# Program order for the way in of every batch, and the second batch's fold on GpSimd, in a long-convolution and mixture-of-experts kernel

## The chip, the core and the metric

The kernel runs on one core of a Trainium2 chip. The metric is the device time of one execution in microseconds (us). The kernel is one launch; its time before the change is the median of three runs.

## The reference

Four batches of 10048 positions and 128 channels go through a gated long convolution, and the result of all 40192 positions goes through a two-level mixture of experts. Cut to what matters:

```
u = x * v
h = (relu(pos_emb @ w1) @ w2) * exp(-0.01 * pos)          # the filter, one per channel
y = irfft(rfft(u, 2S) * rfft(h, 2S), 2S)[:, :S]           # causal convolution over positions
rows = (x * y).reshape(B * S, D)
# mixture of experts: 4 groups x 4 experts, hidden width 1024
g = argmax(rows @ w_group);  e = argmax(rows @ w_expert[g])
out[row] = p(g) * p(e) * (relu(rows @ w1[g, e]) @ w2[g, e])
```

All inputs and outputs are float32.

## The kernel before

The Fourier transforms are written as matrix products over a factorized length, so that TensorE does them. A loop `b = 0 … 4` runs over the batches, and each turn has two stages.

The **row stage** of turn `b` does two things side by side. The *way in* is the forward transform of batch `b`: 43 parts of 3 channels (42 of 3, one of 2). For each part SyncE loads a tile `xv` that holds x and v (288 KB, line 454), VectorE multiplies them in place (`product`, line 459), the halves `lo` and `hi` of the product are folded into `eo` = (lo + hi, lo − hi) (`fold`), 24 matmuls make `psa` from `eo` (line 406), and ScalarE copies `psa` out as `z` and `zr` (line 417). The *way out* is the inverse transform of batch `b − 1`: groups of 12 channels are transposed by TensorE (`pt`, lines 693 and 696), copied by ScalarE (`tt`, line 698), multiplied (`po`, lines 708 and 729), copied by ScalarE (`oo`, lines 738 and 739), then VectorE makes `yt` (line 744) and, with the loaded gate `xo`, `xy` (line 746). One group of 12 channels together with four parts of the way in is called a cycle here; a stage has 10.67 cycles. Turn 0 has only a way in, turn 4 only a way out. Turns 1, 2 and 3 have both; their row stages are called stage 1, 2 and 3.

The **middle** of turn `b` then multiplies batch `b`'s spectrum by the filter's, frequency by frequency: `psb` (TensorE), products `t` on VectorE (lines 654, 657), sum and difference `y` on GpSimd (lines 655, 658), `pbp` on TensorE (line 670).

Into turns 2, 3 and 4 the routing of earlier rows is woven: many small VectorE operations (lines 759 to 1050) that find each row's place, and row scatters on GpSimd (`prow`, line 372), with clears of unused places (line 387). GpSimd's scatters and clears are made to wait for a recent ScalarE copy, which paces them. After turn 4 come the experts' matmuls, which sort no further rows.

The fold of batch 0 is two GpSimd operations, or one on GpSimd and one on VectorE. For batches 1 to 3 ScalarE first writes −hi behind hi into the `xv` tile (line 470), and then one VectorE operation over 384 columns makes both halves (line 472):

```
both = self.minus.pop(d0)
nc.scalar.activation(both[:, :, 128:192], hi, AF.Copy, scale=-1.0)
signed = both[:, :, 64:192].rearrange("p d (j q) -> p d j q", j=2)
nc.vector.tensor_tensor(eo..., bc(lo, 2, 2), signed, ALU.add)
```

The source runs the products three to four parts and the folds three parts ahead of the matmuls (`run_ahead`, `AHEAD = 3`). There are 5 tiles for loads (`NLOAD`) and 5 for `eo` (`NPROD`). So a load for a part can start when the fold of the part five before it has read its tile.

The order of instructions on each engine comes from a scheduler, which places an operation by its own priorities and not where the source has it. `in_turn` overrides it: an operation given to it is kept on its engine right behind the operation that the source wrote before it. It adds an order, no wait. Before, this holds for batch 0 alone.

Of the kernel before, what the change touches and what calls it, by code (L numbers as in the profile page):

```python
# [15 lines left out]
AF = mybir.ActivationFunctionType  # L16
ALU = mybir.AluOpType
# [107 lines left out]
def bc(ap, axis, n):  # L125

    ap = ap.unsqueeze(axis)
    shape = list(ap.shape)
    shape[axis] = n
    return ap.broadcast_to(shape)  # L130
# [18 lines left out]
class Kernel:  # L149
# [280 lines left out]

    def in_turn(self, b, ins):

        if b == 0:
            self.tc.keep_in_program_order(ins)

    def product(self, b, d0, n):
# [25 lines left out]
    def fold(self, xt, b, d0, n):  # L462

        nc = self.nc
        eo = self.ap.tile([NR, GD, 128], F32, tag="prod", name="eo", bufs=NPROD)
        lo, hi = xt[:, :, 0:64], xt[:, :, 64:128]
        odd = d0 // GD % 2
        if b:
            both = self.minus.pop(d0)
            nc.scalar.activation(both[:, :, 128:192], hi, AF.Copy, scale=-1.0)  # L470
            signed = both[:, :, 64:192].rearrange("p d (j q) -> p d j q", j=2)
            nc.vector.tensor_tensor(
                eo[:, :n].rearrange("p d (j q) -> p d j q", j=2), bc(lo, 2, 2), signed, ALU.add
            )
            return b, eo, d0, n, False

        self.in_turn(b, nc.gpsimd.tensor_tensor(eo[:, :n, 0:64], lo, hi, ALU.add))
        sub = nc.vector if d0 >= FIRST and odd else nc.gpsimd
        self.in_turn(b, sub.tensor_tensor(eo[:, :n, 64:128], lo, hi, ALU.subtract))
        return b, eo, d0, n, d0 // GD % 5 == 4 or d0 // GD == 41  # L480
# [968 lines left out]
```

## Time and profile before

| what | before |
|---|---|
| median of three runs | 2063.18 us (2059.78 to 2067.74) |
| the profiled execution's own time | 2065.51 us |
| its span, first to last instruction | 2063.6 us |
| TensorE busy | 1919.7 us, 93% of the span |
| VectorE, ScalarE, GpSimd busy | 78%, 70%, 64% |
| stages 1, 2, 3 (249.98 to 358.21, 462.31 to 579.15, 690.98 to 809.53) | 108.23, 116.84, 118.55 us |
| the middles behind them | 104.10, 111.83, 102.63 us |
| last way out and experts (from 912.16) | to the end of the span |

The stages are read from the first transpose or the last back product of one stretch to that of the next. PE is TensorE, PEld its weight loads, DVE is VectorE, ACT is ScalarE, POOL is GpSimd, SP is SyncE; a "q" behind the name is the engine's own queue of DMA issues. The rows name a waiting instruction, then what it waited for.

### The profile page before, as it was taken

How to read it: one execution, taken by the hardware profiler on the slowest of the kernel's cores; microseconds unless marked ns; L12 is line 12 of the kernel's file. 1: busy time of each engine (PE TensorE's matmuls, PEld its weight loads, DVE VectorE, ACT ScalarE, POOL GpSimd, SP SyncE). 2: the span in 40 equal slices, each digit the busy share in tenths (PEclk: the TensorE clock that was granted, in tenths of full speed). 3: DMA queues.
4: the chain of work that ended last, by engine and by line, in shares of the span. 5: the costliest groups of instructions: out<-in, count | busy, mean ns of one | idle time of the engine just before them, and what ended most of it. 6: DMA issues, size and time to landing. Idle time of an engine off the chain costs nothing.

```text
span 2063.6 us, 53237 instructions
## 1 busy us (share of the span) xinstructions
PE 1919.7 (93%) x17518; PEld 1764.7 (86%) x17518; DVE 1604.0 (78%) x3462; ACT 1441.7 (70%) x3395; POOL 1320.7 (64%) x1371
## 2 busy tenths in 40 slices
PE   8988988977899789988899999999999999999997
PEld 7867877766777577767699999999999999999997
DVE  5587765687558875794699998889999998888885
ACT  6652377436743476446687888888888888888886
POOL 3247600674689657977167777888888885555554
PEclk9999999999999899999899999999999999999999
DMA  4699955976899578968444445455555544444442
GB/s 137 225 264 260 286 159 171 329 237 173 224 308 297 165 211 268 338 204 272 166 144 136 141 151 158 150 191 163 154 163 153 166 144 128 135 124 124 129 124 65
DMA packets 258717, 388.71 MB, mean 188 GB/s; under 512 B 32679, under 2 KB 132754, under 8 KB 258432
## 3 DMA queue, kind: packets, MB, share of 16 engines
q1 hardware_dynamic: 225024, 317.84, 51.3%
q0 software_dynamic: 23904, 51.83, 7.1%
q10 hardware_dynamic: 9504, 15.54, 2.7%
q8 instruction: 142, 2.33, 0.5%
q14 instruction: 143, 1.17, 0.2%
HBM read 303.08 MB, written 83.04 MB: 187 GB/s over the span
## 4 chain that ended last, share of the span: by engine, by line
PE 66%; DMA 8%; DVE 8%; POOL 5%; issue 4%; ACT 4%; SPq 1%; ACTq 0%; DVEq 0%; POOLq 0%
PE py L1318 7%; PE ph L1299 7%; PE ph L1297 7%; PE py L1316 7%; PE py L1317 7%; PE ph L1298 7%; PE psb L488 6%; DMA xv<-xv_in 5%; PE pbp L670 4%; PE psa L406 2%; PE ptm L1330 2%; PE px L1254 2%; PE ptr L811 2%; PE plt L819 1%; PE pt L696 1%
## 5 line engine op out<-in xcount | busy, mean ns | idle before, releaser
L1306 DVE SCALAR_TENSOR_TENSOR hl<-ph,hh 128x512 fp32r<-128x512 f32 x656 | 445.2, 683 | 93.4 <-ACT hh L1305 92.8
L1305 ACT ACTIVATE hh<-ph 128x512 fp32r<-128x512 f32 x656 | 395.7, 603 | 138.6 <-PE ph L1299 73.6
L372 POOL DMA_INDIRECT prow<-stg,adr x316 | 348.0, 1101 | 137.5 <-issue 60.2
L1342 POOL DMA_INDIRECT out<-os,to x328 | 349.0, 1064 | 91.5 <-issue 71.7
L1316 PE MATMUL py<-hh,wh 128*128 128x256 f32 x1312 | 398.6, 304 | 0.0
L1297 PE MATMUL ph<-xh,wh 128*128 128x256 f32 x1312 | 373.6, 285 | 5.1 <-DVE hl L1306 2.7
L1318 PE MATMUL py<-hh,wl 128*128 128x256 f32 x1312 | 373.2, 284 | 5.5 <-POOL wl L1286 5.5
L1299 PE MATMUL ph<-xh,wl 128*128 128x256 f32 x1312 | 373.5, 285 | 0.4 <-DVE wl L1286 0.4
L1298 PE MATMUL ph<-xl,wh 128*128 128x256 f32 x1312 | 373.0, 284 | 0.0
L1317 PE MATMUL py<-hl,wh 128*128 128x256 f32 x1312 | 371.4, 283 | 0.0
L1286 POOL TENSOR_TENSOR wl<-ws,wh 128x512 fp32r<-128x512 f32 x162 | 221.1, 1365 | 203.5 <-ACT wh L1279 202.3
L1318 PEld LDWEIGHTS py<-hh,wl 128*128 128x128 f32 x1312 | 251.4, 192 | 8.4 <-POOL wl L1286 8.3
L1297 PEld LDWEIGHTS ph<-xh,wh 128*128 128x128 f32 x1312 | 252.9, 193 | 5.8 <-ACT hh L1305 2.8
L1299 PEld LDWEIGHTS ph<-xh,wl 128*128 128x128 f32 x1312 | 253.3, 193 | 0.9 <-DVE wl L1286 0.8
L1298 PEld LDWEIGHTS ph<-xl,wh 128*128 128x128 f32 x1312 | 253.2, 193 | 0.1
L1317 PEld LDWEIGHTS py<-hl,wh 128*128 128x128 f32 x1312 | 252.7, 193 | 0.0
L1316 PEld LDWEIGHTS py<-hh,wh 128*128 128x128 f32 x1312 | 252.0, 192 | 0.0
L1286 DVE TENSOR_TENSOR wl<-mw,wh 128x512 fp32r<-128x512 f32 x328 | 237.3, 724 | 0.0
L655 POOL TENSOR_TENSOR y<-t 128x256 f32<-128x256 f32 (+1 forms) x160 | 120.1, 751 | 156.2 <-DVE t L654 152.0
L1279 ACT CAST wh<-mw 128x512 fp32r x328 | 206.6, 630 | 0.0
L1279 ACT CAST wh<-ws 128x512 fp32r<-128x512 f32 x328 | 205.6, 627 | 1.4 <-DMA ws<-m_w 1.4
L670 PE MATMUL pbp<-y,bp 128*128 128x256 f32 x632 | 169.7, 394 | 26.2 <-POOL y L658 25.6
(237 smaller groups left out, 4094.6 us busy)
## 6 DMA issues: line engine op xcount, KB each, us to landing
ws<-m_w SPq DMA_DIRECT2D x328, 256.0 KB
ht<-hspec SPq DMA_DIRECT2D x156, 256.0 KB
xv<-xv_in SPq DMA_DIRECT2D x131, 288.0 KB
bt<-c_b SPq DMA_DIRECT2D x95, 256.0 KB
xg<-prow SPq DMA_DIRECT2D x164, 130.0 KB
bp<-c_bp SPq DMA_DIRECT2D x76, 256.0 KB
stg<-xyd SPq DMA_DIRECT2D x76, 256.0 KB
xyd<-xy SPq DMA_DIRECT2D x57, 256.0 KB
```

The lines of the kernel that those rows point to most:

```text
L372: ins = self.nc.gpsimd.indirect_dma_start(self.d["prow"], bass.IndirectOffsetOnAxis(ap=u.adr[:, t : t + 1], axis=0), u.rows[:, t - u.t0], ...
L1279: k.fix(k.nc.scalar.copy(hi, self.matrix(i, half, self.ea)))
L1286: ins = v.tensor_tensor(lo, self.matrix(i, half, self.ed), self.wh[i][half].bitcast(F32), ALU.subtract)
L1297: k.fix(nc.tensor.matmul(ph[:, j], wh, self.xh, start=True, stop=False))
L1298: k.fix(nc.tensor.matmul(ph[:, j], wh, self.xl, start=False, stop=False))
L1299: k.fix(nc.tensor.matmul(ph[:, j], wl, self.xh, start=False, stop=True))
L1305: k.fix(nc.scalar.activation(hh, ph, AF.Relu))
L1306: k.fix(nc.vector.scalar_tensor_tensor(hl, ph, 0.0, hh.bitcast(F32), ALU.max, ALU.subtract))
L1316: k.fix(nc.tensor.matmul(self.py, wh, self.hh[c], start=(c == 0), stop=False))
L1317: k.fix(nc.tensor.matmul(self.py, wh, self.hl[c], start=False, stop=False))
L1318: k.fix(nc.tensor.matmul(self.py, wl, self.hh[c], start=False, stop=(c == NC - 1)))
L1342: ins = k.nc.gpsimd.indirect_dma_start(k.d["out"], bass.IndirectOffsetOnAxis(ap=self.to[:, h : h + 1], axis=0), o[:, h], None, bounds_chec ...
```

## The change

`in_turn` keeps program order for every batch, and not for batch 0 alone (the filter's own way in stays out). So the products and the copies `z` and `zr` of batches 1, 2 and 3 are now pinned. For batch 1 the fold becomes two GpSimd operations of 96 × 192 each (86 in all), with no ScalarE negation and no VectorE fold. For batches 2 and 3 the fold stays as it was, and its two operations are pinned too.

```diff
@@ in_turn
-        if b == 0:
+        if b != "h":
             self.tc.keep_in_program_order(ins)
@@ fold
+        if b == 1:
+            nc.gpsimd.tensor_tensor(eo[:, :n, 0:64], lo, hi, ALU.add)
+            nc.gpsimd.tensor_tensor(eo[:, :n, 64:128], lo, hi, ALU.subtract)
+            return b, eo, d0, n, False
         if b:
             both = self.minus.pop(d0)
-            nc.scalar.activation(both[:, :, 128:192], hi, AF.Copy, scale=-1.0)
+            self.in_turn(b, nc.scalar.activation(both[:, :, 128:192], hi, AF.Copy, scale=-1.0))
             signed = both[:, :, 64:192].rearrange("p d (j q) -> p d j q", j=2)
-            nc.vector.tensor_tensor(
+            ins = nc.vector.tensor_tensor(
                 eo[:, :n].rearrange("p d (j q) -> p d j q", j=2), bc(lo, 2, 2), signed, ALU.add
             )
+            self.in_turn(b, ins)
             return b, eo, d0, n, False
```

From the fold on, lines of the changed kernel are 5 higher (`yt` is line 749, `xy` 751, `tt` 703, `oo` 743 and 744); VectorE's fold moves from 472 to 476, the negation from 470 to 474, and GpSimd's new operations are lines 469 and 470.

**VectorE in the steady part of stage 2.** Numbers mark the tiles: `xv_6584` is a part's load tile, `eo` its fold. Before:

```order
761 L459 TENSOR_TENSOR xv_6584<-xv_6584 96x3x128
762 L472 TENSOR_TENSOR eo_6549<-xv_6522 96x384
763 L459 TENSOR_TENSOR xv_6632<-xv_6632 96x3x128
764 L459 TENSOR_TENSOR xv_6687<-xv_6687 96x3x128
765 L459 TENSOR_TENSOR xv_6708<-xv_6708 96x3x128
766 L744 TENSOR_TENSOR yt_6519<-po_6488,oo_6516 128x474
767 L472 TENSOR_TENSOR eo_6587<-xv_6546 96x384
768 L746 TENSOR_TENSOR xy1_5766<-yt_6519,xo_6502 128x79x6
769 L472 TENSOR_TENSOR eo_6635<-xv_6584 96x384
770 L472 TENSOR_TENSOR eo_6690<-xv_6632 96x384
```

The same place after the change:

```order
711 L459 TENSOR_TENSOR xv_6419<-xv_6419 96x3x128
712 L476 TENSOR_TENSOR eo_6422<-xv_6381 96x384
713 L459 TENSOR_TENSOR xv_6470<-xv_6470 96x3x128
714 L476 TENSOR_TENSOR eo_6473<-xv_6419 96x384
715 L749 TENSOR_TENSOR yt_6519<-po_6488,oo_6516 128x474
716 L751 TENSOR_TENSOR xy1_5766<-yt_6519,xo_6502 128x79x6
717 L459 TENSOR_TENSOR xv_6522<-xv_6522 96x3x128
718 L476 TENSOR_TENSOR eo_6525<-xv_6470 96x384
```

Before, three products stand in a row ahead of `yt`, and the folds that free load tiles stand behind it. After, product and fold alternate, and around the same `yt_6519` the products stand at an earlier part (`xv_6470` where `xv_6708` stood).

**ScalarE in a cycle of stage 1.** Before, from one set of `tt` copies to the `oo` copies of the same cycle:

```order
L698 COPY tt<-pt 128x512 x3
L470 ACTIVATE xv<-xv 96x3x64 x2
L417 COPY z<-psa 128x128x3
L417 COPY zr<-psa 128x3x30
L724 DMA xo<-x_out 128x474
L470 ACTIVATE xv<-xv 96x3x64 x2
L724 DMA xo<-x_out 128x474
L738 ACTIVATE oo<-po 64x474
```

After:

```order
L703 COPY tt<-pt 128x512 x3
L729 DMA xo<-x_out 128x474
L417 COPY z<-psa 128x128x3
L417 COPY zr<-psa 128x3x30
L743 ACTIVATE oo<-po 64x474
```

The negations are gone from stage 1, and with them ScalarE's waits on products there.

**GpSimd where the middle of turn 0 ends and stage 1 starts** (a piece of the difference; `y` is the middle's last sum and difference, `wr` to `iota` are four small constant loads):

```order
 L663 TENSOR_TENSOR y<-t_2945 128x2x128
+L469 TENSOR_TENSOR eo<-xv 96x3x64
 L660 TENSOR_TENSOR y<-t_2957 128x128
+L470 TENSOR_TENSOR eo<-xv 96x3x64
+L469 TENSOR_TENSOR eo<-xv 96x3x64
 L663 TENSOR_TENSOR y<-t_2960 128x128
 L193 DMA wr<-w_router 128x32
```

Three of the new operations stand ahead of the last `y`, on which the stage's first transposes depend.

**VectorE where stage 2 starts, after the change** (lines 955 to 983 are routing, in four passes; in the third and fourth, lines 964 to 977 between 961 and 981 run on GpSimd, so that line 981 waits for GpSimd):

```order
L981 TENSOR_REDUCE other<-f 128x79
L983 TENSOR_TENSOR pos<-pos,other 128x79
L955 SCALAR_TENSOR_TENSOR f<-keep,oh 128x316
L956 TENSOR_TENSOR oh<-oh,c_5586 128x4
L459 TENSOR_TENSOR xv<-xv 96x3x128 x5
L476 TENSOR_TENSOR eo<-xv 96x384 x4
L749 TENSOR_TENSOR yt<-po,oo 128x474
```

Before the change these five products stand one by one among the routing operations ahead of this place; now they stand together behind them.

## Rows read from the trace of the kernel before

**Rows 1.** The page: lines on the chain that ended last, with shares.

```profile
PE py L1318 7%; PE ph L1299 7%; PE ph L1297 7%; PE py L1316 7%; PE py L1317 7%; PE ph L1298 7%; PE psb L488 6%; DMA xv<-xv_in 5%; PE pbp L670 4%; PE psa L406 2%; PE ptm L1330 2%; PE px L1254 2%; PE ptr L811 2%; PE plt L819 1%; PE pt L696 1%
```

**Rows 2.** Windows: stages 1 to 3: us, PE, PEld, DVE, ACT, POOL busy, clock, DMA, GB/s.

```profile
249.98:358.21 108.23, 94.03 (x1442) 83.20 (x1441) 66.00 (x122) 84.23 (x212) 1.47 (x3) 0.98 0.62 169
...
462.31:579.15 116.84, 98.95 (x1442) 86.12 (x1441) 73.33 (x157) 84.25 (x210) 67.89 (x72) 0.93 0.73 205
...
690.98:809.53 118.55, 105.08 (x1444) 90.02 (x1444) 79.72 (x181) 83.08 (x210) 72.22 (x74) 0.89 0.71 204
```

**Rows 3.** Windows of single cycles: one of stage 1, three of stage 2.

```profile
303.12:311.76 8.64, 8.63 (x137) 7.65 (x135) 5.05 (x10) 6.92 (x19) 0.00 (x0) 1.00 0.71 195
...
480.92:495.86 14.94, 10.16 (x137) 8.62 (x136) 10.16 (x27) 11.46 (x30) 3.26 (x3) 0.77 0.59 175
495.86:505.16 9.30, 8.64 (x137) 7.66 (x136) 5.07 (x10) 5.55 (x15) 4.37 (x6) 1.00 0.86 226
505.16:519.61 14.45, 10.16 (x137) 8.64 (x136) 7.66 (x15) 10.48 (x26) 7.88 (x9) 0.88 0.73 192
```

**Rows 4.** Waits in stage 2: us in total, times, longest.

```profile
DVE xv L459 <- DMA xv<-xv_in: 28.2, 24, 3.0
ACT xv L470 <- DVE xv L459: 20.9, 19, 4.4
...
PE pt L696 <- ACT tt L698: 17.7, 9, 4.8
```

**Rows 5.** Waits in stage 1.

```profile
DVE xv L459 <- DMA xv<-xv_in: 28.5, 31, 3.0
ACT xv L470 <- DVE xv L459: 18.9, 22, 1.8
...
PE pt L696 <- ACT tt L698: 13.2, 8, 2.2
```

**Rows 6.** SyncE's own waits, stage 1 (line 454 issues the loads).

```profile
SPq L454 <- DVE eo L472: 71.9, 30, 5.8
...
SPq L454 <- DMA xv<-xv_in: 1.4, 1, 1.4
```

**Rows 7.** Timeline of stage 2: start, us, engine, line, operation, [idle before <- releaser].

```profile
507.42 0.55 DVE L459 TENSOR_TENSOR xv<-xv 96x384 f32<-96x384 f32 x1 [2.71 <-DMA xv<-xv_in]
...
510.61 1.50 ACT L698 COPY tt<-pt 128x384 f32<-128x384 f32 x3
...
511.16 1.02 PE L696 MATMUL pt<-ident,z 128*128 128x128 f32 x4 [4.29 <-ACT tt L698]
...
514.01 0.55 DVE L472 TENSOR_TENSOR eo<-xv 96x384 f32<-96x384 f32 x1 [1.41 <-PE psa L406]
...
518.44 0.55 DVE L459 TENSOR_TENSOR xv<-xv 96x384 f32<-96x384 f32 x1 [2.59 <-DMA xv<-xv_in]
```

**Rows 8.** Groups by line and shape over the span: busy us, mean ns | idle before.

```profile
L459 DVE TENSOR_TENSOR xv<-xv 96x384 f32<-96x384 f32 x126 | 71.8, 570 | 75.0 <-DMA xv<-xv_in 74.1 <-issue 0.4
L472 DVE TENSOR_TENSOR eo<-xv 96x384 f32<-96x384 f32 x126 | 70.0, 566 | 23.5 <-PE psa L406 16.7 <-POOL y L658 4.3 <-ACT xv L470 2.4
...
L470 ACT ACTIVATE xv<-xv 96x192 f32<-96x192 f32 x126 | 45.3, 365 | 74.8 <-DVE xv L459 68.5 <-issue 1.7 <-ACT zr L417 1.4
...
L477 POOL TENSOR_TENSOR eo<-x 96x192 f32<-96x192 f32 x37 | 26.6, 733 | 21.7 <-DVE x L459 20.5 <-PE psa L406 1.2
...
L746 DVE TENSOR_TENSOR xy<-yt,xo 128x474 f32<-128x474 f32 x60 | 38.9, 648 | 0.9
...
L477 POOL TENSOR_TENSOR eo<-xv 96x192 f32<-96x192 f32 x5 | 3.0, 590 | 0.0
```

**Rows 9.** Timeline, GpSimd, where stage 3 starts.

```profile
683.10 1.38 POOL L387 DMA_INDIRECT prow<-empty,fidx  x1 [2.47 <-ACT xv L470]
684.50 4.74 POOL L658 TENSOR_TENSOR y<-t 128x128 f32<-128x128 f32 x1
```

**Rows 10.** Timeline, TensorE, the last back product ahead of stage 3.

```profile
689.30 1.22 PE L670 MATMUL pbp<-y,bp 128*128 128x256 f32 x2 [7.89 <-POOL y L658]
```

## Prediction

> **What bounds the kernel now.** The page's chain is mostly TensorE, but one link is of another kind: 5% of the span, some 103 us, runs through the load of `xv` [rows 1]. Those loads belong to the way in of turns 0 to 3, so the place to look is the three stages in which a way in and a way out run side by side. The windows of these stages show TensorE busy for 94.03 of 108.23, 98.95 of 116.84 and 105.08 of 118.55 us [rows 2]: 14, 18 and 13.5 us idle, and in the later two some more lost because the granted clock falls (0.93, 0.89). One cycle undisturbed takes 8.64 us with TensorE busy for 8.63 of it; in stage 2 cycles of 14.94 and 14.45 us alternate with one of 9.30 [rows 3]. In the long ones TensorE's own work has grown to 10.16 us, the same 137 matmuls at a clock of 0.77 or 0.88: it first waits, then runs slowly.
>
> What it waits for is in the waits: TensorE's `pt` waits for ScalarE's `tt`, 17.7 us in stage 2; ScalarE's negation waits 20.9 us for VectorE's product, and the product 28.2 us for its load [rows 4]. Read from the bottom up that is one chain, since ScalarE works in order: a negation that waits holds up the `tt` copies behind it. Stage 1 shows the same with 13.2, 18.9 and 28.5 us [rows 5]. The timeline of one long cycle has it in sequence: the product at 507.42 came 2.71 us late, the `tt` copies started at 510.61, and `pt` resumed at 511.16 after 4.29 us [rows 7].
>
> Is the load late because the DMA is slow or because it is issued late? SyncE, which issues the loads, spends 71.9 us of stage 1 waiting for VectorE's fold (line 472), which frees a load tile, and 1.4 us for an earlier load [rows 6]. In the timeline a fold runs at 514.01 and the product at 518.44 gets its data after waiting 2.59 us [rows 7]: 4.4 us from a freed tile to a used one. So the tile is freed too late. VectorE's order explains it: three products stand in a row, each needing a new tile, while the folds that would free tiles stand behind them and behind `yt`.
>
> **The change part by part.**
>
> *Products and folds in program order (batches 2, 3).* It adds no operation and no wait. Product and fold alternate, so each freed tile is followed by its load, which now has about four parts, one cycle of 8.64 us [rows 3], until its product: twice the 4.4 us that it takes. I expect the product's waits for its load to go, with them most of the negation's and `pt`'s. What is late next: in order, `yt` waits for `oo`, and a product behind it waits too, but it is ahead by three parts. The DMA share rises: the same bytes in 102 instead of 116.84 us make 0.84 of 0.73 [rows 2]. A cycle with 0.86 ran in 9.30 us [rows 3], so I take not 8.64 but 9.2 us a cycle: 10.67 × 9.2 = 98.2 us. Bounds: 8.64 a cycle (92.2) and the mean of a long and a short cycle, (14.45 + 9.30) / 2 = 11.9, nothing gained.
>
> *The start of stages 2 and 3.* Before, the first five products and folds lay under the end of the middle, among routing. Now VectorE has the five products together behind its routing, and the first four folds behind them, so the way in starts later: five products and a first fold of 0.57 us [rows 8] are 3.4 us, unless the way out's own transposes cover them. I take +3.5 us in stage 2 (from +1 to +10). In stage 3 the first matmuls of the way in stand still further back, so +5 (from +2 to +10). So stage 2 becomes 98.2 + 3.5 = 101.7, that is −15; stage 3 98.2 + 5 = 103.2, −15.
>
> *Batch 1's fold on GpSimd.* It removes 43 ScalarE negations of 365 ns, 15.7 us, and 43 VectorE folds of 566 ns, 24.3 us [rows 8], and adds 86 GpSimd operations. An operation of this shape on `xv` takes 590 ns with no neighbour on VectorE and 733 ns beside VectorE's products [rows 8]: 50.7 to 63.0 us of GpSimd, which had 1.47 us in this stage [rows 2]. So GpSimd has room. ScalarE falls from 84.23 to about 68.5 us, and no longer stands between a product and `tt`, so `pt`'s 13.2 us of waits [rows 5] should mostly go. I take 9.0 us a cycle, 96 us, and 4 us at the start (three of the new operations stand ahead of the last `y`, 3 × 0.59 = 1.8 us, and I add as much again for the other folds, which the four constant loads hold up): 100 us, −8. Bounds: 92.2 + 2 = 94 and 108.
>
> GpSimd and VectorE slow each other, and this decides how good that is. `y` (128 × 128) took 4.74 us at 684.50 [rows 9] where VectorE ran operations with two inputs one behind the other; and 590 became 733 ns. If they exclude each other fully, the demand in stage 1 is 86 × 590 ns + 43 products × 570 ns + 22 `xy` × 648 ns = 50.7 + 24.5 + 14.3 = 89.5 us of 100 [rows 8]: it fits, without much to spare. This is where the Trainium skill speaks against the change: "SBUF — State Buffer", section "Who interferes with whom", says that a VectorE operation with two inputs in SBUF and a GpSimd operation that reads SBUF use one port pair, of which the first to issue holds the whole. The trace agrees (4.74 us for `y`). By that rule alone the sum is the 89.5 us just worked out, under the stage's 100, and stage 1 keeps its gain.
>
> *Ends of the middles.* At the start of stage 3 the last `y` stands on GpSimd behind a clear that came 2.47 us late, then starves itself [rows 9]; TensorE stood for 7.89 us [rows 10]. After the change the products and folds of the next batch no longer crowd VectorE there, so the `y` should take near its usual time of under a microsecond: 4 us. I count −3 for both ends together (from 0 to −7), since part of it is the late start counted above.
>
> **The sum.** −8 − 15 − 15 − 3 = −41. The profiled execution took 2065.51 us, so 2024.5. The median of the runs is 2.33 us lower (2063.18): about 2022. What comes after the last stage keeps its order and its time. 0.5% is 10.3 us.
>
> **The rivals.**
>
> *A: stage 1 gains nothing and the starts eat more.* If GpSimd is slowed to the 733 ns and VectorE is held in turn, the demand is 63.0 + 24.5 + 14.3 = 101.8 us in stage 1 plus the lags between product and fold: 108 as before, no gain; with starts of +6.5 and +8, stages 2 and 3 gain 12 each. With nothing from the middles' ends that is −24: 2041.5, or about 2039 as a median. For it: batch 0's folds on GpSimd took 733 ns beside products [rows 8]. Against it: GpSimd may lag by three parts before a matmul waits.
>
> *B: the load is slow by itself.* Then an earlier issue helps little, the product's waits of 28 us a stage [rows 4, 5] stay, and only the middles' ends gain: 2063.18 − 4, about 2059, no change that can be measured. For it: the DMA share is 0.73 in stage 2 [rows 2], and shorter stages push it up. Against: SyncE's own waits [rows 6].
>
> *C: slower, by the starts of stages 2 and 3.* VectorE is strictly in order there. Its routing waits for GpSimd, GpSimd's clears wait for a ScalarE copy (2.47 us here for a negation [rows 9]), and ScalarE's first copies of the new stage wait for matmuls whose folds now stand behind that routing. In such a ring nothing overlaps; a start then costs the whole middle's end again, the 7.89 us [rows 10] plus 3.4 and the clears' 1.38 each [rows 9], some 13 us for each of two stages, 26 in all. It decides the sign where the steady cycles gain less than that together; with a third of the forecast's 41 us, 14, it gives 2063 + 26 − 14 = 2075. Against: the first `tt`, `po` and `oo` of the way out need none of this.
>
> **How the numbers follow.** The forecast, about 2022, has a chance of 0.62; A 0.20, B 0.10, C 0.08. Better than forecast is bounded by 8.64 us a cycle and small starts: 92.2 + 2 in stage 1, 92.2 + 1 and + 2 in the others, −14 − 23.6 − 24.4 = −62, or 2001. The range of 2000 to 2051 takes in the forecast and A and leaves out B and C, together 0.18. Faster by over 0.5% has the forecast and A, 0.82; within 0.5% is B, 0.10; slower is C, 0.08.
>
> **What would show it.** Right: stages of about 100, 102 and 103 us; the product's waits for its load under 10 us a stage; no wait of `pt` for `tt` over 1 us in the steady part; granted clock near 1.0 in stages 2 and 3; GpSimd's folds between 590 and 733 ns. Wrong in the first step: product waits near 28 us with loads issued a cycle ahead (B). Wrong on stage 1: `psa` waiting for GpSimd's folds throughout (A). Wrong on the starts: TensorE idle for over 10 us where stages 2 and 3 begin (C). It would be faster than I think if the clock stays full and the middles, which I leave as they are, gain as well.

## The result and the profile after

The change took the median from 2062.12 us (2059.78 to 2067.74, four runs) to 2030.48 us (2027.63 to 2035.0, four runs): a ratio of 0.9845, 95% interval 0.9816 to 0.9873. 31.6 us were gained where 41 were forecast; the span fell from 2063.6 to 2030.3 us. The sign and the mechanism of the steady part held; one term of the sum was badly wrong, and it hides behind a total that looks nearly right.

The windows of the profile after, by nearly the same marks as [rows 2] and with the middles between them, have the columns us, PE, PEld, DVE, ACT and POOL busy with instructions, clock, DMA share, GB/s:

```profile
248.64:346.72 98.08, 97.30 (x1443) 84.59 (x1443) 49.10 (x80) 72.17 (x172) 56.26 (x87) 0.98 0.66 180
346.72:446.45 99.73, 92.15 (x575) 73.70 (x576) 80.71 (x191) 39.69 (x93) 68.28 (x91) 0.97 0.87 288
446.45:552.70 106.25, 98.26 (x1442) 86.26 (x1442) 77.15 (x152) 82.76 (x216) 65.61 (x71) 0.97 0.83 233
552.70:659.95 107.25, 94.09 (x577) 73.20 (x578) 82.56 (x188) 40.21 (x94) 93.50 (x120) 0.98 0.89 292
659.95:779.00 119.05, 108.81 (x1445) 93.53 (x1445) 84.46 (x182) 82.27 (x214) 67.09 (x73) 0.89 0.75 207
```

Read against the stages of before, 108.23, 116.84 and 118.55 us, and the middles of 104.10 and 111.83:

| part | before | after | gained | forecast |
|---|---|---|---|---|
| stage 1 | 108.23 | 98.08 | 10.2 | 8 |
| stage 2 | 116.84 | 106.25 | 10.6 | 15 |
| stage 3 | 118.55 | 119.05 | −0.5 | 15 |
| middles of turns 1 and 2 | 104.10, 111.83 | 99.73, 107.25 | 9.0 | 3 |
| all before, between and behind these | 1504.05 | 1499.94 | 4.1 | 0 |

The last row is the span less the others; of its 4.1 us 1.3 lie ahead of stage 1 and 2.8 behind stage 3. The marks differ a little: before, stages 1 and 2 start at the first `psa`, after the change at the last back product. From the first transpose to the middle's first `psb`, the marks used below, stage 1 gained 9.6 and stage 2 11.1 us. So stage 1 and the steady parts are as forecast or better, the middles' ends gave three times what was forecast, and stage 3 gave nothing. Single cycles in the steady part of stages 1, 2 and 3, by the windows of the profile after:

```profile
295.30:304.35 9.05, 9.05 (x137) 7.85 (x136) 4.93 (x9) 6.69 (x16) 5.36 (x8) 1.00 0.70 184
500.81:509.88 9.07, 8.89 (x137) 7.92 (x136) 6.19 (x12) 8.29 (x22) 7.08 (x9) 1.00 1.00 289
745.56:754.59 9.03, 9.03 (x137) 7.85 (x136) 6.63 (x14) 6.98 (x20) 6.45 (x8) 1.00 0.95 263
```

All three are alike, 137 matmuls in 9.03 to 9.07 us at the full clock, where [rows 3] had 14.94 and 9.30 in turn. In stage 2 the waits that [rows 4] showed are nearly gone:

```profile
ACT xv L474 <- DVE xv L459: 10.7, 6, 5.9
...
PE pt L701 <- ACT tt L703: 1.6, 5, 0.5
...
DVE xv L459 <- DMA xv<-xv_in: 0.8, 2, 0.6
```

28.2 us of waiting for loads are 0.8, 17.7 us of `pt` waiting for `tt` are 1.6; of the negation's 10.7 us, 5.9 are one wait at the stage's start. But where stage 3 starts, another set of waits stands (the waits of 659.95 to 779.00):

```profile
POOL prow L387 <- ACT zr L417: 15.8, 1, 15.8
...
PE psa L406 <- DVE eo L476: 6.2, 2, 5.4
...
DVE lt L970 <- POOL f L967: 5.1, 2, 3.3
```

The timeline shows how they hang together:

```profile
659.95 0.90 PE L698 MATMUL pt<-ident,zr 128*128 128x128 f32 x3 [0.47 <-ACT zr L686]
...
670.73 2.42 DVE L459 TENSOR_TENSOR xv<-xv 96x384 f32<-96x384 f32 x5
...
677.74 1.75 POOL L387 DMA_INDIRECT prow<-empty,fidx  x1 [15.76 <-ACT zr L417]
...
682.48 0.49 DVE L970 TENSOR_TENSOR lt<-f,thr 128x316 f32<-128x316 f32 x1 [3.27 <-POOL f L967]
...
683.45 1.59 DVE L459 TENSOR_TENSOR xv<-xv 96x384 f32<-96x384 f32 x1
...
689.45 0.55 DVE L476 TENSOR_TENSOR eo<-xv 96x384 f32<-96x384 f32 x1
...
690.14 5.17 PE L406 MATMUL psa<-fa,eo 96*64 96x158 f32 x48 [5.38 <-DVE eo L476]
```

The way out starts at 659.95. (`psa` x48 are four parts: the trace has 12 matmuls a part, 512 in a stage.) The first products come 10.8 us later, because they stand behind the routing on VectorE. The first `zr` copy of the new stage therefore comes late, and a clear on GpSimd waits 15.76 us for it. Behind the clear stand GpSimd's routing passes, VectorE waits for those, and the next product (683.45) waits behind VectorE's wait. The next fold (689.45) comes behind more of VectorE's own routing, and TensorE stands 5.38 us for it. Two windows price it:

```profile
659.95:727.08 67.13, 58.13 (x680) 48.94 (x680) 48.46 (x115) 37.26 (x96) 29.05 (x31) 0.80 0.58 160
727.08:779.00 51.92, 50.68 (x768) 44.59 (x766) 36.00 (x68) 45.01 (x119) 38.04 (x43) 1.00 0.97 267
```

The second is the steady part: 768 matmuls in 51.92 us. At that pace the first window's 680 are 46.0 us, so the start loses 21.1 us. TensorE stood idle for 9.0 us of the first window, and its own matmuls took longer, at a clock of 0.80. In stage 2 the first two groups of the way out took 25.67 us for 2 × 9.05, 7.6 us lost.

### The profile page after: what moved, and what is told of

The parts are those of the page before. It is cut to its first block, busy times and chain, and to the rows that moved or that the text cites. A ratio compares the mean times of both kernels' runs of the same rounds, so it can differ in the third digit from the quotient of the medians.

```text
span 2030.3 us, 53326 instructions
## 1 busy us (share of the span) xinstructions
PE 1917.5 (94%) x17518; PEld 1762.2 (87%) x17518; DVE 1590.7 (78%) x3419; ACT 1422.8 (70%) x3352; POOL 1360.0 (67%) x1457
## 4 chain that ended last, share of the span: by engine, by line
PE 49%; DVE 2%; POOL 2%; ACT 1%; issue 1%; DMA 0%; ACTq 0%; DVEq 0%; POOLq 0%
PE py L1323 7%; PE py L1321 7%; PE py L1322 7%; PE ph L1304 7%; PE ph L1302 7%; PE ph L1303 7%; PE ptm L1335 2%; PE px L1259 2%; POOL wl L1291 1%; POOL out L1347 1%; PE po L713 0%; PE po L734 0%; PE ptr L816 0%; PE pt L701 0%; DVE wl L1291 0%
## 5 line engine op out<-in xcount | busy, mean ns | idle before, releaser
L372 POOL DMA_INDIRECT prow<-stg,adr x316 | 343.6, 1087 | 119.7 <-issue 55.6
L406 PE MATMUL psa<-fa,eo 96*64 96x158 f32 x2048 | 187.5, 313 | 22.7 <-DVE eo L476 11.8
L683 ACT COPY z<-pbp 128x512 f32<-128x512 f32 x128 | 74.7, 585 | 164.0 <-PE pbp L675 159.4
```

Of the source, the lines that this page charges most:

```text
L372: ins = self.nc.gpsimd.indirect_dma_start(self.d["prow"], bass.IndirectOffsetOnAxis(ap=u.adr[:, t : t + 1], axis=0), u.rows[:, t - u.t0], ...
```

## The experiments

Each is compared with runs of the kernel before that stand beside it. Stages are given from the first transpose to the middle's first `psb`; so counted, before had 106.32, 116.16 and 118.55 us and the changed kernel 96.77, 105.08 and 119.05.

**e1: the order alone.** Batch 1's fold is again ScalarE's negation and VectorE's one operation, pinned like those of batches 2 and 3.

```diff
-        if b == 1:
-            nc.gpsimd.tensor_tensor(eo[:, :n, 0:64], lo, hi, ALU.add)
-            nc.gpsimd.tensor_tensor(eo[:, :n, 64:128], lo, hi, ALU.subtract)
-            return b, eo, d0, n, False
```

> Batches 1 to 3 in program order, but batch 1's fold as before (ScalarE negation, one VectorE operation). If the order is what made stage 1 faster, stage 1 runs at about 9.05 us a cycle as the steady parts of stages 2 and 3 do after the change, first transpose to the middle's first product in 96 to 100 us, and the time is 2028 to 2034 us. If the fold on GpSimd is what made it, stage 1 stays near 106 us and the time is about 2040 us.

2030.41 us against 2061.25, a ratio of 0.9845 (0.9829 to 0.9862): the whole gain. Its stage 1 in the windows:

```profile
248.89:345.90 97.01, 95.51 (x1441) 83.99 (x1441) 65.26 (x123) 81.18 (x214) 0.92 (x2) 1.00 0.67 183
```

97.0 us with GpSimd all but idle (0.92 us). The fold on GpSimd adds nothing that can be measured to the order.

**e2: GpSimd's fold alone.** The other half: `in_turn` again for batch 0 only.

```diff
-        if b != "h":
+        if b == 0:
             self.tc.keep_in_program_order(ins)
```

> Batch 1's fold on GpSimd, program order for batch 0 alone as before. If the order is what made stage 1 faster, products still stand three in a row ahead of yt and stage 1 gains at most half of its 9.5 us: 2057 to 2063 us. If the fold on GpSimd is enough (ScalarE has no negation left that waits), stage 1 is about 97 us and the time 2050 to 2054 us.

2082.41 us, a ratio of 1.0081 (1.0057 to 1.0106): slower than before, outside both expectations. Stage 1 took 123.25 us. Its waits:

```profile
POOL eo L469 <- PE psa L406: 63.9, 23, 5.9
DVE xv L459 <- DMA xv<-xv_in: 28.1, 11, 5.3
...
DVE xv L459 <- POOL eo L469: 19.0, 5, 5.3
PE pt L701 <- ACT tt L703: 18.5, 9, 3.1
ACT oo L743 <- DVE xy L751: 16.4, 5, 4.0
```

No negation is left, and `pt` still waits 18.5 us for `tt`. The products wait for loads and, now, for GpSimd; `yt` and `xy` wait behind them on VectorE, `oo` waits for `xy`, and `tt` stands behind `oo` on ScalarE. GpSimd's fold waits for an `eo` tile, so the folds are as far ahead as their tiles allow. By these waits the products stand too far ahead in VectorE's order, rather than the data too far behind. And to take the negations out is not enough by itself.

**e3: the first parts free.** The change, but the first five products, negations and folds of batches 2 and 3 are not pinned.

```diff
-    def in_turn(self, b, ins):
+    def in_turn(self, b, ins, d0=D):
 
-        if b != "h":
+        if b != "h" and (b < 2 or d0 >= FIRST):
             self.tc.keep_in_program_order(ins)
```

(`d0` is passed for products, negations and folds.)

> The change, but the first five products, negations and folds of batches 2 and 3 are not pinned, so that they lie among the routing at the end of the middle as before. If the lost gain is the start of stages 2 and 3 (7.6 and 22 us over the steady cycles), because the way in stands behind the routing there, most of it comes back: 2008 to 2022 us, stage 3's first 45 us of work in under 55. The rival says that the routing and GpSimd's clears hold the start whatever the first parts do: 2027 to 2033 us.

2025.08 us against 2061.25, 0.9818 (0.979 to 0.9846): 5 us below the changed kernel where 8 to 22 were expected, and the intervals overlap. The windows, two middles and the stages behind them, say why:

```profile
347.52:452.42 104.90, 94.03 (x584) 74.89 (x584) 81.41 (x189) 42.14 (x99) 71.48 (x91) 0.95 0.87 287
452.42:555.34 102.92, 96.93 (x1435) 84.85 (x1434) 73.76 (x154) 80.24 (x209) 64.39 (x71) 0.97 0.82 227
555.34:664.82 109.48, 94.16 (x578) 72.95 (x578) 85.93 (x187) 41.77 (x99) 98.64 (x120) 0.95 0.89 296
664.82:771.23 106.41, 100.28 (x1444) 88.04 (x1444) 81.45 (x181) 80.84 (x210) 68.65 (x72) 0.95 0.77 220
```

Stage 3 gained 12.6 us and stage 2 2.2, but the middles, 100.90 and 107.25 us by these marks in the changed kernel, gave 6.2 back. At stage 3 the last back product of the middle shows it, first in the changed kernel and then here (before it waited 7.89 us [rows 10]):

```profile
658.78 0.70 PE L675 MATMUL pbp<-y,bp 128*128 128x256 f32 x2 [2.80 <-POOL y L663]
```

```profile
663.13 1.22 PE L675 MATMUL pbp<-y,bp 128*128 128x256 f32 x2 [6.95 <-POOL y L663]
```

So the early products cost at the middles' ends 6.2 of the 14.8 us that they save in the stages; that is the gain of the middles in the table above, read from the other side. The span is 4.9 us shorter, not 8.6: 2.9 us are lost behind stage 3 and 0.8 ahead of stage 1, and why was not looked into.

**e4: the clears wait for the middle.** Order and work of the changed kernel, but a clear waits for the last copy of a back product and not for the newest copy of the way in.

```diff
-            self.pace = nc.scalar.copy(self.z[:, k0 : k0 + n], po[:, :n])
+            self.pace = self.paced = nc.scalar.copy(self.z[:, k0 : k0 + n], po[:, :n])
...
-                self.tc.add_manual_dep(ins.ins, self.pace.ins.name, kind, reason="one step at a time")
+                self.tc.add_manual_dep(ins.ins, (self.pace if u else self.paced).ins.name, kind, reason="one step at a time")
```

(the copy of `zr` in the same way)

> The change, but the clears of unused places wait for the middle's last copy of a back product and not for the newest copy of the way in; order and work are the same. If the ring (clear waits 15.8 us for the new stage's first copy, GpSimd's routing stands behind the clear, VectorE's routing waits for GpSimd, the next products stand behind that) is what costs the start, the clear's wait goes and 5 to 15 us come back: 2015 to 2025 us. If the products' place behind VectorE's own routing is the whole of it, the time is that of the change, 2028 to 2033 us.

2023.57 us, 0.9818 (0.9797 to 0.9839). Stage 2 and stage 3 in the windows:

```profile
447.07:552.26 105.19, 97.69 (x1441) 85.83 (x1441) 74.69 (x147) 81.61 (x214) 63.74 (x71) 0.97 0.83 232
659.67:765.92 106.25, 101.39 (x1444) 88.58 (x1444) 83.97 (x179) 81.98 (x214) 67.28 (x73) 0.97 0.82 233
```

Stage 3 fell from 119.05 to 106.25 us and its clock rose from 0.89 to 0.97; stage 2, where the clear waited only 7.6 us, stayed. One wait of a clear is thus most of stage 3's loss. e1, where a clear waited 16.5 us at the same place, had 116.72 us in its stage 3. The medians differ by 7 us where stage 3 differs by 12.8; in this profile the span differs by 9.8, as 3.3 us are lost behind stage 3. The intervals of the two ratios overlap, so the stage's window, of one profiled execution each, is the better evidence.

**e5 to e8: which of the pinned operations.** These four ran on another chip than the other experiments, where the kernel before itself took 2126.31 us, so only ratios and stage 1 are used; three of the kernels were run again below. e5 is e1 with only the products pinned, e6 its complement (`not product`), e7 is e1 with the clears of e4, and e8 is e7 with all routing passes on VectorE. The edit of e5, then that of e8:

```diff
-    def in_turn(self, b, ins):
+    def in_turn(self, b, ins, product=False):
 
-        if b != "h":
+        if b == 0 or b != "h" and product:
             self.tc.keep_in_program_order(ins)
```

```diff
-            w = v if b >= self.nbat - 2 or h < 2 else nc.gpsimd
+            w = v
```

> Old fold in all batches; of batches 1 to 3 only the products are kept in program order, not negations, folds and copies of psa. If what hurt was a product standing too far ahead on VectorE, in front of yt and of the folds that free its own load tile, this alone gives the steady gain: cycles of 9.0 to 9.3 us in all three stages, 2028 to 2040 us. If the place of the negations on ScalarE (in front of the tt copies) is what hurt, cycles stay near 10 to 11.5 us: 2050 to 2063 us.

> The complement: negations, folds and copies of batches 1 to 3 in program order, products not. By the first theory products can still stand ahead of yt (in stage 2 up to three between two yt, alternating with folds), so loads are still waited for and at most half of the 31 us comes: 2045 to 2063 us. By the second theory most of the gain is here: 2028 to 2040 us.

> Old fold, program order in all batches, and the clears wait for the middle's last copy. If batch 1's fold on GpSimd is worth nothing here too and the clears' wait costs what it cost before, this is the time of the changed kernel with the clears moved: 2020 to 2027 us, stage 3 at 105 to 108 us. If the fold on GpSimd helps somewhere, it is 3 us or more above that.

> As the kernel before this one, and all four routing passes on VectorE, so that VectorE does not wait for GpSimd where stages 2 and 3 start. If that wait (4.8 us in stage 2) holds the first products, stage 2's first two cycles shrink from 25.9 us towards 20: 2010 to 2020 us. If VectorE's added work of some 6 operations of 0.48 us in each turn costs as much as the wait, 2020 to 2027 us.

Ratios: e5 0.9964 (0.9926 to 1.0002), e6 0.9878 (0.9802 to 0.9954), e7 0.9997 (0.9956 to 1.0038), e8 0.9974 (0.9945 to 1.0003). Stage 1 took 104.0 us in e5 and 97.1 us in e6, e7's 97.0 and e8's 97.0 were those of e1: against my first theory, the negations, folds and copies together carried the gain of stage 1, and the products' order alone brought little of it. Stages 2 and 3 took 128 to 149 us in all four, why they are longer there stays open, and nothing is drawn from them. It also limits what follows: e12 below is the kernel of e8 and has a ratio of 0.9774, against 0.9974 here. Order and pacing together gained nothing on that chip that can be measured (e7, e8). What is said of stages 2 and 3 is therefore shown for one chip only; the changed kernel itself was not run on the other.

**e9 and e10: the same two halves again.**

> The kernel of e6 again, beside undisturbed runs of the kernel before. Its stage 1 took 97.1 us although products still waited 16.1 us for loads: so the negation's place on ScalarE carries the gain, and the products' own waits cost nothing. By this theory stages 2 and 3 gain as well, at 9.0 to 9.3 us a cycle, and since the products lie among the routing as before, their starts lose less than the changed kernel's: 2010 to 2030 us. If the products' order matters in stages 2 and 3, 2035 to 2060 us.

> The kernel of e5 again, beside undisturbed runs. Its stage 1 took 104.0 us at 9.9 us a cycle, with pt still waiting 7.1 us for tt. By the theory of the negation's place all three stages stay near 10 us a cycle, starts late as in the changed kernel: 2045 to 2070 us. If the products' order carries part of it in stages 2 and 3, 2030 to 2045 us.

e9: 2040.27 us against 2065.39, 0.9871 (0.985 to 0.9893). e10: 2048.7 us, 0.9917 (0.9899 to 0.9935). The windows of stages 1 to 3, e9 first:

```profile
249.90:347.45 97.55, 96.15 (x1440) 83.57 (x1440) 64.94 (x123) 80.80 (x214) 0.93 (x2) 1.00 0.66 183
450.68:561.61 110.93, 101.23 (x1440) 86.28 (x1440) 71.79 (x142) 80.72 (x214) 67.42 (x72) 0.95 0.79 222
667.47:789.12 121.65, 110.08 (x1444) 92.82 (x1444) 82.42 (x189) 81.54 (x214) 74.53 (x74) 0.89 0.72 204
```

And e10:

```profile
252.03:354.52 102.49, 95.06 (x1431) 82.79 (x1431) 63.20 (x118) 83.14 (x209) 0.00 (x0) 1.00 0.62 167
456.66:569.94 113.28, 101.19 (x1441) 87.61 (x1441) 74.81 (x147) 85.07 (x214) 64.63 (x72) 0.92 0.78 216
675.31:791.75 116.44, 101.73 (x1444) 87.76 (x1444) 84.04 (x179) 83.97 (x214) 68.31 (x73) 0.95 0.76 211
```

The waits of e9, in stage 1, and then in stage 2:

```profile
DVE xv L459 <- DMA xv<-xv_in: 17.1, 18, 2.1
DVE yt L745 <- ACT oo L740: 14.4, 17, 2.4
...
ACT oo L739 <- DVE eo L472: 3.4, 8, 0.8
...
PE pt L697 <- ACT tt L699: 1.0, 3, 0.5
```

```profile
DVE xv L459 <- DMA xv<-xv_in: 28.4, 25, 2.5
...
ACT oo L739 <- DVE eo L472: 10.4, 8, 2.7
...
DVE yt L745 <- ACT oo L740: 8.9, 8, 2.1
...
PE pt L697 <- ACT tt L699: 7.4, 6, 2.3
```

And of e10, in stage 1:

```profile
PE pt L697 <- ACT tt L699: 7.2, 8, 1.1
...
DVE xv L459 <- DMA xv<-xv_in: 1.9, 1, 1.9
```

In e9's stage 1 the products still wait 17.1 us for loads, and it runs at 9.0 to 9.5 us a cycle all the same. By its waits, a wait for a load costs nothing there because it is over before the next link of the way out behind it on VectorE has its own data: `yt` still waits for `oo` 17 times. In its stage 2 the products wait 28.4 us, as long as before; `yt` waits for `oo` only 8 times, ScalarE waits 10.4 us for VectorE in front of `oo` where it waited 3.4, `pt`, whose copies stand behind `oo`, waits again, and cycles lie between 9.0 and 12.9. That is the second expectation of e9: in stages 2 and 3 the products' order matters. In e10 the waits for loads are gone (1.9 us in stage 1), but `pt` waits 7.2 us for `tt`, and the cycles of the steady parts stand at 9.9 us, as its first expectation had them. Each half leaves one blocked queue. The halves' gains, 25 and 17 us, don't add up to the 31 of both; no run here says why.

**e11: products free, clears paced by the middle.** e9's kernel with e4's edit.

> As e9 (old fold; negations, folds and copies in program order, products free), and the clears wait for the middle's last copy. If the late start comes from products behind the routing and from the clears' wait, both are gone here: stage 3 at 100 to 105 us, 2005 to 2020 us, below the changed kernel and below e4. If free products make stages 2 and 3 uneven again, 2025 us or more.

2042.69 us, 0.9878 (0.9855 to 0.99): no better than e9, its stage 3 at 118.6 us. The first expectation fell and the second held: where the products are free, the cycles stay uneven, from 9.0 to 16.9 us in stage 3. How much of that is the start and how much the steady part was not separated.

**e12: everything in order, clears paced by the middle, no pass on GpSimd.** e8's kernel again.

> The kernel of e8 again: old fold, everything in program order, clears paced by the middle, all routing passes on VectorE. If VectorE's wait for GpSimd's passes still holds the starts, 2010 to 2020 us and stage 2's first two cycles near 20 us instead of 25.9. If not, 2020 to 2030 us as in e4.

2017.9 us against 2065.39, 0.9774 (0.9759 to 0.979), an interval that lies wholly below that of the change. Stages 2 and 3:

```profile
447.88:551.16 103.28, 97.75 (x1441) 86.12 (x1441) 76.10 (x153) 81.96 (x214) 60.44 (x65) 0.97 0.84 237
658.71:763.44 104.73, 100.93 (x1444) 87.86 (x1445) 84.11 (x191) 82.10 (x214) 58.32 (x61) 0.99 0.85 234
```

Stages 2 and 3 are 1.9 and 1.5 us shorter than in e4, and stage 2's first two cycles took 24.0 us, not the 20 that I expected: GpSimd's passes are a small part of the start. In the profiles another 3.4 us of its gain over e4 lie behind stage 3, which was not looked into. It is the fastest version tried, and uses no GpSimd fold.

## Why the prediction was right in sign and short by a quarter

*The bound, and the steady part: right.* In-order queues were the limit, not the DMA: with the DMA share at 0.95 to 1.00 in cycles of 9.03 and 9.07 us, loads still come in time. Cycles of 9.05 us stand where I took 9.0 and 9.2. Rival B, the load slow by itself, is out: with products in order 0.8 us of 28.2 are left.

*The chain that I read: right at its ends, too simple in between.* I read load, product, negation, `tt`, `pt` as one chain whose first link is the late load. e9 shows a stage whose loads are waited for 17.1 us without harm, e10 one whose loads are in time and which still loses 0.9 us a cycle. What costs is a waiting operation that stands in front of a link of the way out and waits longer than that link's own data do: a negation in front of `oo` and `tt` on ScalarE, a product in front of `yt` on VectorE. The change all but removes both waits. That it is the negation, and not the folds or copies that e9 pins with it, is read from the waits; no run pinned it alone.

*Batch 1's fold on GpSimd: right in size, wrong in cause.* I credited 8 us to ScalarE's lost negations; stage 1 gained 10.2, but e1 has the same stage with the negations back. By itself the GpSimd fold loses (e2). My price for it held: between 590 and 733 ns were forecast, and the groups of stage 1 in the changed kernel show

```profile
L470 POOL TENSOR_TENSOR eo<-xv 96x192 f32<-96x192 f32 x41 | 28.0, 682 | 0.0
...
L459 DVE TENSOR_TENSOR xv<-xv 96x384 f32<-96x384 f32 x37 | 22.1, 636 | 0.0
```

against the products of e1 in the same stage, with GpSimd idle:

```profile
L459 DVE TENSOR_TENSOR xv<-xv 96x384 f32<-96x384 f32 x37 | 20.3, 549 | 0.0
```

Both engines pay: 682 for 590 ns [rows 8], 636 for 549 ns. (The 590 ns had a neighbour, against my reading: VectorE was at work on the filter through nearly all of those five folds, at 87 to 94 us, but on no products.) `xy`, with two inputs in SBUF, rose from 653 to 707 ns on average, its longest from 654 to 965; `yt`, with one of its inputs in PSUM, stayed at 652 for 649. Rival A's place was real and its price too small to matter. That agrees with the Trainium skill, "SBUF — State Buffer", section "Who interferes with whom", by which a VectorE operation with two inputs in SBUF contends with a GpSimd operation that reads SBUF.

*The starts: the step that failed.* "+3.5 us in stage 2" was 7.6, inside its bounds of 1 and 10; "+5" in stage 3, with bounds of 2 and 10, was 21.1. Rival C had described the place and the mechanism, the ring of VectorE's routing, GpSimd's clears and the first copies of the new stage, priced at some 13 us a stage; I gave it 0.08 because the way out's first steps need none of it. They do not, and they ran: three groups of the way out were done by 683.7 us, but beside them only five parts of the way in where twelve belong. That does not help, since the stage ends when the slower of the two ends. The terms +3.5 and +5 counted the products and folds behind VectorE's routing and nothing for the clear's wait and what stands behind it; e4 takes that wait out and 12.8 of stage 3's us come back. I also left the clock out of both prices, and the start ran at 0.80. Of the other 8 us e12 gives back 1.5; the rest no run takes apart.

*Ends of the middles: right, and under-sized.* 9.0 us were gained, the forecast was 3 (from 0 to 7). The last `y` ahead of stage 3 took 0.47 us, where it had taken 4.74 [rows 9]. e3 puts the first products back among the routing there and loses 6.2 of it.

So of 41 us, 20 did not come from stages 2 and 3, and 12 came on top, in the span, from the middles (6), stage 1 (2) and what lies outside (4).

## What to carry to other kernels

On an in-order engine ask of each waiting instruction what stands behind it and could run sooner, not only how long it waits: 17.1 us of VectorE's waits were free in e9's stage 1, while 7.2 us of `pt`'s waits in e10 are 0.9 us in each cycle. Pinning an order makes a steady loop even, but look at the seams: here the first iterations had run early under the tail of the stage before, and the pinned order brought them late. A pacing wait that takes "the newest copy" changes its meaning when that copy moves; tie it to the stage that it is meant to pace.

## What the runs showed that I had not expected

A late start costs TensorE twice. The first 680 matmuls of stage 3 took 67.13 us in the changed kernel, with 9.0 us idle and a granted clock of 0.80. In e12 nearly the same number, in the same mix, stands in 53.89 us at 0.98:

```profile
658.71:712.60 53.89, 50.58 (x679) 43.32 (x679) 47.38 (x122) 38.00 (x96) 17.14 (x17) 0.98 0.67 184
```

Of the 13.2 us between them 5.7 are idle time (9.0 against 3.3) and 7.6 are the matmuls themselves (58.13 against 50.58): the work behind the waits cost more than the waits.

And moving work to an engine that had 1.47 us to do in a stage made that stage 16.9 us longer, as long as the order around it was not fixed (e2, 106.32 to 123.25).
